# Gate products with the tokens as the stationary operand

## The chip, the core and the metric

The kernel runs on one core of one Trainium2 chip. The metric is the device time of one execution in microseconds. Five engines work side by side on a core, each through its own list of instructions in order: TensorE (PE, matrix products, with its weight loads shown apart as PEld), VectorE (DVE), ScalarE (ACT), GpSimd (POOL) and SyncE (SP, which issues DMAs). A matrix product holds one operand still in the array (the stationary one, which a weight load brings there) and streams the columns of the other through it. Before the change the median of three runs is 1689.38 us, from 1689.24 to 1691.82.

## The reference

Causal attention over 4 batches and 8 heads of 576 tokens, with a bias from cumulative sums; its output, 2304 tokens of 512 features, goes through a mixture of 8 experts whose weights per token come from gate logits that are balanced over rows and columns (Sinkhorn steps):

```
x = attn_out.transpose(0, 2, 1, 3).reshape(2304, 512)
logits = x @ w_gate                      # 512 x 8
P = exp(logits - logits.max())
repeat 8 times: P /= rows' sums; P /= columns' sums; P *= N / E
out = sum over e of P[:, e] * (relu(x @ w1[e]) @ w2[e])
```

## The kernel before

The program has two stages. In the attention stage, up to about 350 us, the 16 pairs of heads are worked off in 80 slots (a pair and a block of 128 query rows, the fifth of 64 rows for both heads). `st0` computes scores (tile `sc`, line 497), their row minimum on DVE (line 506) and the exponential on ACT (tile `T`, line 538); `st1` normalises `T` on ACT (line 560); `st2` transposes it on PE (tile `tr`, lines 569 and 579) and copies it out on DVE (lines 574 to 580); `st3` multiplies with v (tile `pv`, line 599). Line 615 on ACT writes its result as the high half of x (tile `xh`) and line 616 on DVE the low half. x is kept transposed, features on the partitions and tokens along the columns, and every value as a pair of a high and a low part.

Between the slots a queue (`Stream`, worked off by `fill`) puts in the first units of expert 0, for which x of a batch must be complete: products of line 148 and line 177, with results in two PSUM banks (tile `g`, taken by `bank`). Into this queue the gate is inserted, for two blocks of tokens per batch, eight blocks in all: six of 256 tokens and two of 384. Weights for the stream are loaded into `wraw` and split by line 110 on ACT (high part) and line 111 on POOL (low part).

The gate (`gate`, lines 620 to 633) has 16 columns in `wg`: the high and the low part of the 8 columns of w_gate. `gate` holds 16 columns of `wg` as the stationary operand and streams 256 or 384 tokens, 4 blocks of features by 2 parts of x, into a bank; ACT copies the 16 x 256 logits to `lt` (line 632). `gate_t` is queued two places later, transposes 16 x 128 pieces of `lt` on PE (line 641), and ACT copies the result to `lraw` (line 646), 128 tokens on the partitions. After the last block the Sinkhorn steps read `lraw` (line 795 on), beside the expert products of the second stage (lines 1024, 1145 and 1202), which take the rest of the time.

The order of the instructions on each engine is not the order of the code: a scheduler plans the whole program with its own estimate of what each instruction costs, and the stages' order on every engine comes out of that plan. The products of line 599 are the only ones with a raised priority.

Of the kernel before, what the change touches and what calls it, by code (L numbers as in the profile page):

```python
# [8 lines left out]
F32 = mybir.dt.float32  # L9
# [5 lines left out]
P = 128  # L15
# [8 lines left out]
KD = DM // P  # L24
# [21 lines left out]
def fused_kernel(ctx: ExitStack, tc: tile.TileContext, qT, kT, v, s, w_gate, wu, out):  # L46
    nc = tc.nc
# [8 lines left out]
    ident = const.tile([P, P], F32, name="ident")  # L56
    ones = const.tile([P, P], F32, name="ones")
    wg = const.tile([P, KD, 16], F32R, name="wg")
# [14 lines left out]
    def xgroup(b):  # L73
        if b not in xg:
            xg[b] = big.tile([P, 2, KD, GW], F32R, name="xh", tag="xh", bufs=2)
        return xg[b]

    def xcols(b, hl, k, n0, n):
        return xgroup(b)[:, hl, k, n0 - GB[b] : n0 - GB[b] + n]
# [57 lines left out]
    def bank():  # L137
        return cur["g"].tile([P, 512], F32, name=cur["gt"], tag=cur["gt"])
# [110 lines left out]
    stream = Stream()  # L249
# [71 lines left out]
    apool = actx.enter_context(tc.tile_pool(name="apool", bufs=1))  # L321
# [7 lines left out]
    def load_head(h):  # L329
        tag, bufs = ("raw", 4) if h else ("T", 7)  # L330
        for which, src in (("q", qT), ("k", kT)):
            r = (h - 2) % 5 - 2 if 2 <= h < 17 else -1
            if r < 0:
                raw = apool.tile([P, S], F32, name=f"raw{which}", tag=tag, bufs=bufs)
            else:
                if not rx:
                    rx.append(stage.tile([P, 6, S], F32, name="rx", tag="w7"))
                raw = rx[0][:, 2 * r + (which == "k")]
            eng = nc.scalar if h < 2 and which == "k" else nc.sync
            eng.dma_start(out=raw[:D], in_=src[h])  # L340
            heads_in[0] = eng.dma_start(out=raw[D:], in_=src[h])
            raws[h, which] = raw
# [139 lines left out]
    def load_v(g):  # L482
        b, hp = divmod(g, NPAIR)
        t = vtt[g % 2]
        src = v[b, :, hp * P : (hp + 1) * P]
        with tc.issue_after(heads_in[0].ins):
            nc.sync.dma_start(
                out=t[:, 0:4, :], in_=src[0:512].rearrange("(c p) d -> p c d", p=P)
            )
            nc.sync.dma_start(out=t[D:, 4, :], in_=src[512:576])  # L490
# [20 lines left out]
    def st0(t, j):  # L511

        g, i = t
        T = apool.tile([P, S], F32, name="T", tag="T", bufs=7)
        mn = apool.tile([P, 2], F32, name="mn", tag="mn", bufs=6)
        if j == 0:
            sums[t] = apool.tile([P, 2], F32, name="sm", tag="sm", bufs=4)
        if i < 4:
            n = (i + 1) * P
            sc = psa.tile([P, 512], F32, name="sc", tag="sc", bufs=3)  # L520
            scores(sc[:, :n], 2 * g + j, i, slice(0, n), True, True)
            m0 = 384 - i * P
            row_min(T[:, :n], sc[:, :n], mask[:, m0 : m0 + n], 3.0e38, mn[:, 1:2])
        else:
            n = S
            for pi in range(2):
                cols = slice(pi * 288, (pi + 1) * 288)
                sc = psa.tile([P, 512], F32, name="sc", tag="sc", bufs=3)
                for jj in range(2):
                    scores(sc[:, :288], 2 * g + jj, 4, cols, jj == 0, jj == 1)  # L530
                row_min(
                    T[:, cols],
                    sc[:, :288],
                    mask2 if pi else mask[:, :288],
                    mn[:, 0:1] if pi else 3.0e38,
                    mn[:, pi : pi + 1],
                )
        nc.scalar.activation(
            T[:, :n], T[:, :n], AF.Exp, bias=mn[:, 1:2], scale=-1.0,
            accum_out=sums[t][:, j : j + 1],  # L540
        )
        Ts[t, j] = T

    def heads(t):
        return range(2 if t[1] < 4 else 1)

    def st1(t):

        g, i = t
        sm = sums.pop(t)  # L550
        nh = len(heads(t))
        n = (i + 1) * P if i < 4 else S
        nc.scalar.activation(
            sm[:, :nh], sm[:, :nh], AF.Identity, bias=guard[:, 0:1], scale=1.0
        )
        rec = apool.tile([P, 2], F32, name="rec", tag="rec", bufs=2)
        nc.vector.reciprocal(out=rec[:, :nh], in_=sm[:, :nh])
        for j in heads(t):
            T = Ts[t, j][:, :n]
            nc.scalar.activation(T, T, AF.Copy, scale=rec[:, j : j + 1])  # L560
# [58 lines left out]

    def gate(b, n0, n):  # L620
        ps = bank()
        for k in range(KD):
            for x in range(2):
                nc.tensor.matmul(  # L624
                    ps[:16, :n],
                    lhsT=wg[:, k, :],
                    rhs=xcols(b, x, k, n0, n),
                    start=(k == 0 and x == 0),
                    stop=(k == KD - 1 and x == 1),
                )  # L630
        lt = apool.tile([16, 384], F32, name="lt", tag="lt", bufs=2)
        nc.scalar.copy(lt[:, :n], ps[:16, :n])
        lts[n0] = lt

    lts = {}

    def gate_t(n0, n):
        lt = lts.pop(n0)
        ps = bank()
        for c in range(n // P):  # L640
            nc.tensor.transpose(
                ps[:, c * 16 : (c + 1) * 16],
                lt[:, c * P : (c + 1) * P],
                ident[:16, :16],
            )
        nc.scalar.copy(
            lraw[:, n0 // P : (n0 + n) // P, :],
            ps[:, : n // P * 16].rearrange("p (c e) -> p c e", e=16),
        )
# [35 lines left out]
    def fill(ti):  # L685

        nxt = min([x for x in (23, 43, 63) if x > ti] + [NS + 3])
        budget[0] += len(stream.queue) / (2.0 * (nxt - ti))
        while budget[0] >= 0.5:
            stream.step()  # L690
            budget[0] -= 1.0
# [19 lines left out]
    for ti in range(NS + 3):  # L711
        if ti < NS:
            g, i = slots[ti]
            if i == 4 and g + 1 < NG:
                load_v(g + 1)
            for j in heads(slots[ti]):
                st0(slots[ti], j)
        if 1 <= ti <= NS:
            st1(slots[ti - 1])
        fill(ti)  # L720
        if 3 <= ti:
            pg, pi = slots[ti - 3]
            if pi == 1:
                st3(pg, (0, 1))
            elif pi == 4:
                st3(pg, (2, 3, 4))
        for j in range(2):
            if 2 <= ti < NS + 2 and j in heads(slots[ti - 2]):
                st2(slots[ti - 2], j)
            if j == 0:  # L730
                fill(ti)
        if ti < NS and i in (1, 3) and g + 1 < NG:
            h = 2 * (g + 1) + i // 2
            prep_head(h)
            ahead = {2: (4, 5), 3: (6,), 16: ()}.get(h, (h + (3 if h < 16 else 2),))
            for hh in ahead:
                if hh < B * H:
                    load_head(hh)
        gs = (ti - 7) // 5
        if ti >= 7 and slots[ti - 7][1] == 4 and gs >= NPAIR:  # L740
            spill(*divmod(gs, NPAIR))
        if ti in (24, 28, 32, 36):
            spill(0, (ti - 24) // 4)
        if ti == 6:
            gate_weights()
        if 4 <= ti < 18:
            u, r = divmod(ti - 4, 7)
            if r in (0, 3):
                with tc.issue_after(heads_in[0].ins):
                    w_load_early(u, (r // 3,))  # L750
            if r > 2:
                w_split_early(u, r - 3)
        prep(ti)
        if ti == 66:
            for i in range(2):
                nc.gpsimd.tensor_copy(
                    xgroup(3)[:, i, :, : EDGE[1] - EDGE[0]],
                    xgroup(2)[:, i, :, GB[3] - GB[2] : GB[3] - GB[2] + EDGE[1] - EDGE[0]],
                )

        for bb in range(B):
            if ti == (bb + 1) * 20 + 2:
                if bb < B - 1:
                    for k in range(4):
                        stream.add_visit(4 * bb + k, w_load_early, w_split_early)
                for x, (n0, n) in enumerate(EARLY[bb]):
                    stream.queue.insert(4 * x + 1, lambda b=bb, n0=n0, n=n: gate(b, n0, n))
                    stream.queue.insert(4 * x + 3, lambda n0=n0, n=n: gate_t(n0, n))
    for hp in range(NPAIR - 2, NPAIR):
        if 20 * (B - 1) + 5 * hp + 4 + 7 >= NS + 3:  # L770
            spill(B - 1, hp)
# [454 lines left out]
    k = 0  # L1226
# [161 lines left out]
```

## Time and profile before

| | |
|---|---|
| median of 3 runs | 1689.38 us |
| the profiled execution | 1689.67 us |
| its span, first to last instruction | 1687.9 us |
| PE busy | 1662.8 us (99%) |
| DVE, ACT, POOL busy | 1175.9, 833.9, 866.8 us |
| mean granted clock of PE | 0.992 of full speed |

Busy times come from records of single instructions. A product's record runs from its start to its modelled end, and the next one starts before that end, so how long a product holds PE is read from the distance between starts. The granted clock is the share of TensorE's full speed, 2.4 GHz, that was let through; it has two levels, 1.00 and 0.50. A row of the timeline gives the start, the time from the first start to the last end of a merged group, the engine, the line, the operation, what is written from what, the sizes, the count, and in brackets how long the engine sat idle before it and what ended that.

### The profile page before, as it was taken

The page shows a single profiled execution, that of the slowest core. Times are in us where ns is not written, and L with a number is a line of the kernel's source. Part 1 is how long each engine was busy: PE and PEld are TensorE (multiplying, and loading weights), DVE is VectorE, ACT ScalarE, POOL GpSimd, SP SyncE. Part 2 cuts the span into 40 slices and gives each one's busy share as a digit, 9 for nine tenths or more (in the row PEclk, how much of TensorE's full clock was granted, in tenths as well). Part 3 has the DMA queues.
Part 4 walks back from the last instruction along what each step waited for, and adds up shares of the span by engine and source line. Part 5 has one row for each costly group of instructions (what it writes and reads, how often), then busy time and mean ns, then how long its engine had stood idle before and what let it go on. Part 6 is the DMA issues. An engine that isn't in the chain of part 4 may idle for free.

```text
span 1687.9 us, 31232 instructions
## 1 busy us (share of the span) xinstructions
PE 1662.8 (99%) x11149; PEld 1568.2 (93%) x11149; DVE 1175.9 (70%) x2307; ACT 833.9 (49%) x1816; POOL 866.8 (51%) x797
## 2 busy tenths in 40 slices
PE   7899999999999999999999999999999999999998
PEld 6788898888899999999899999999999999999998
DVE  6677566665866766776457777777777778777666
ACT  5876766633544444444235444444445444444443
POOL 7658868432653554553314545554554555455543
PEclk8899999999999999999999999999999999999999
DMA  7677666283876866865966566666687666665652
GB/s 199 176 217 233 197 176 193 98 321 132 289 251 232 266 218 214 280 216 190 354 183 206 183 191 188 188 188 188 189 313 241 210 190 187 187 187 184 188 186 88
DMA packets 204699, 351.06 MB, mean 208 GB/s; under 512 B 21056, under 2 KB 102976, under 8 KB 204512
## 3 DMA queue, kind: packets, MB, share of 16 engines
q1 hardware_dynamic: 204064, 348.14, 64.5%
q8 instruction: 89, 1.46, 0.4%
q10 hardware_dynamic: 480, 0.92, 0.2%
q14 instruction: 66, 0.54, 0.1%
HBM read 248.89 MB, written 94.81 MB: 204 GB/s over the span
## 4 chain that ended last, share of the span: by engine, by line
PE 90%; DVE 4%; DMA 2%; ACT 1%; POOL 1%; issue 1%; SPq 1%; ACTq 0%; DVEq 0%; POOLq 0%
PE c L1024 34%; PE zz L1145 13%; PE zz L1202 13%; PE y L1202 10%; PE g L148 4%; PE g L177 4%; PE pv L599 3%; PE sc L497 3%; PE tr L569 2%; PE c L177 1%; PE c L148 1%; DVE s L999 1%; DMA wraw<-wu 1%; DVE h L252 1%; PE g L624 0%
## 5 line engine op out<-in xcount | busy, mean ns | idle before, releaser
L252 POOL TENSOR_TENSOR w2o<-r,w2o 128x512 fp32r<-128x512 f32 x189 | 272.4, 1462 | 282.0 <-ACT w2o L1182 273.4
L1202 PE MATMUL zz<-w2o,h 128*128 128x256 f32 x2016 | 272.8, 280 | 0.0
L1024 PE MATMUL c<-xS,w1o 128*128 128x384 f32 x1344 | 271.5, 336 | 1.0 <-ACT t L1039 0.6
L1202 PEld LDWEIGHTS zz<-w2o,h 128*128 128x128 f32 x2016 | 263.2, 188 | 0.2 <-POOL w2o L252 0.2
L1145 PE MATMUL zz<-w2p,h 128*128 128x512 f32 x1008 | 256.8, 391 | 0.4 <-ACT h L987 0.4
L988 DVE SCALAR_TENSOR_TENSOR h<-z,h 128x384 fp32r<-128x384 f32 x252 | 192.5, 769 | 66.0 <-ACT h L987 63.3
L987 ACT ACTIVATE h<-z 128x384 fp32r<-128x384 f32 x252 | 130.6, 525 | 205.3 <-DVE z L255 201.4
L1024 PEld LDWEIGHTS c<-xS,w1o 128*128 128x128 f32 x1344 | 227.3, 188 | 2.5 <-DVE z L255 1.2
L999 DVE SCALAR_TENSOR_TENSOR s<-z,s 128x384 f32<-128x384 f32 x224 | 180.4, 843 | 65.2 <-ACT s L1062 62.0
L252 POOL TENSOR_TENSOR h<-s,h 128x384 fp32r<-128x384 f32 x112 | 138.0, 1240 | 165.5 <-ACT h L995 164.8
L1145 PEld LDWEIGHTS zz<-w2p,h 128*128 128x128 f32 x1008 | 186.9, 188 | 29.5 <-ACT h L987 0.7
L1024 PE MATMUL c<-x,w1o 128*128 128x384 f32 x1008 | 202.9, 336 | 0.0
L1202 PE MATMUL y<-w2o,h 128*128 128x256 f32 x1512 | 201.7, 280 | 0.7 <-DVE a L1128 0.6
L1202 PEld LDWEIGHTS y<-w2o,h 128*128 128x128 f32 x1512 | 194.6, 188 | 1.5 <-DVE a L1128 1.0
L255 DVE TENSOR_TENSOR z<-c,t 128x384 f32<-128x384 f32 x252 | 136.7, 550 | 69.6 <-PE c L1024 65.5
L1024 PEld LDWEIGHTS c<-x,w1o 128*128 128x128 f32 x1008 | 170.5, 188 | 0.5
L1128 DVE SCALAR_TENSOR_TENSOR a<-zz,prob,a 128x256 f32<-128x256 f32 (+1 forms) x210 | 110.6, 530 | 67.1 <-PE zz L1202 52.4
L995 ACT CAST h<-s 128x384 fp32r<-128x384 f32 x224 | 110.9, 513 | 74.0 <-DVE s L999 69.0
L1024 PE MATMUL c<-xS,wp 128*128 128x384 f32 x672 | 134.5, 336 | 1.4 <-DVE z L255 1.4
L1182 ACT CAST w2o<-r 128x1024 fp32r<-128x1024 f32 x98 | 102.5, 1047 | 52.9 <-PE y L1202 39.5
L1024 PEld LDWEIGHTS c<-xS,wp 128*128 128x128 f32 x672 | 119.0, 188 | 9.6 <-DVE z L255 2.7
L252 POOL TENSOR_TENSOR wp<-s,wp 128x512 fp32r<-128x512 f32 x56 | 80.2, 1432 | 84.1 <-ACT wp L914 76.1
(149 smaller groups left out, 2727.5 us busy)
## 6 DMA issues: line engine op xcount, KB each, us to landing
w1o<-w1d SPq DMA_DIRECT2D x392, 256.0 KB
w1d<-wp SPq DMA_DIRECT2D x84, 512.0 KB
r<-wu SPq DMA_DIRECT2D x70, 512.0 KB
r<-w2d SPq DMA_DIRECT2D x56, 512.0 KB
sa<-wu SPq DMA_DIRECT2D x28, 512.0 KB
w2d<-sb SPq DMA_DIRECT2D x56, 256.0 KB
wraw<-wu SPq DMA_DIRECT2D x20, 512.0 KB
xS<-xd_S SPq DMA_DIRECT2D x12, 768.0 KB
```

The costliest lines, as they stand in the source:

```text
L148: nc.tensor.matmul(ps[:, :n], lhsT=w1[:, w, o : o + P], rhs=xcols(b, x, k, n0, n), start=(k == 0 and t == 0), stop=(k == KD - 1 and t == 2),)
L252: (eng or nc.gpsimd).tensor_tensor(out=out, in0=a, in1=b, op=ALU.subtract)
L255: (eng or nc.gpsimd).tensor_tensor(out=out, in0=a, in1=b, op=ALU.add)
L987: mark["a"] = nc.scalar.activation(t[:, 0], z, AF.Relu)
L988: mark["v"] = nc.vector.scalar_tensor_tensor(out=t[:, 1], in0=z, scalar=0.0, in1=t[:, 0].bitcast(F32), op0=ALU.max, op1=ALU.subtract,)
L995: nc.scalar.copy(t[:, 0], z)
L999: nc.vector.scalar_tensor_tensor(out=out, in0=z, scalar=0.0, in1=other, op0=ALU.max, op1=op)
L1024: mm = nc.tensor.matmul(ps, lhsT=w[:, wl, k], rhs=x[:, xl, k], start=(fresh and k == 0 and t == 0), stop=(k == 1 and t == 2), skip_group_c ...
L1128: nc.vector.scalar_tensor_tensor(out=a, in0=ps, scalar=prob[:, c, e : e + 1], in1=a, op0=ALU.mult, op1=ALU.add)
L1145: mm = nc.tensor.matmul(zb[ci], lhsT=h[:, a, ci * P : (ci + 1) * P], rhs=w[:, b_], start=(ui == 0 and f == 0 and t == 0), stop=(ui == UPE ...
L1182: nc.scalar.copy(w[:, :, 0], r)
L1202: nc.tensor.matmul(ps, lhsT=h[:, a, ci * P : (ci + 1) * P], rhs=w[:, ui, b_], start=(fresh and ui == 0 and t == 0), stop=(ui == UPE - 1 an ...
```

## The change

The operands of the gate's products change places: 128 tokens of x are the stationary operand, and the 16 columns of `wg` are streamed. The result has the tokens on the partitions already, so `lt`, its copy and the transposes go, and one copy per block brings the logits to `lraw`. In place of 8 products for a block there are 8 for each 128 tokens. The second entry in the queue goes too.

```diff
     def gate(b, n0, n):
         ps = bank()
-        for k in range(KD):
+        for c in range(n // P):
             for x in range(2):
-                nc.tensor.matmul(
-                    ps[:16, :n],
-                    lhsT=wg[:, k, :],
-                    rhs=xcols(b, x, k, n0, n),
-                    start=(k == 0 and x == 0),
-                    stop=(k == KD - 1 and x == 1),
-                )
-        lt = apool.tile([16, 384], F32, name="lt", tag="lt", bufs=2)
-        nc.scalar.copy(lt[:, :n], ps[:16, :n])
-        lts[n0] = lt
-
-    lts = {}
-
-    def gate_t(n0, n):
-        lt = lts.pop(n0)
-        ps = bank()
-        for c in range(n // P):
-            nc.tensor.transpose(
-                ps[:, c * 16 : (c + 1) * 16],
-                lt[:, c * P : (c + 1) * P],
-                ident[:16, :16],
-            )
+                for k in range(KD):
+                    nc.tensor.matmul(
+                        ps[:, c * 16 : (c + 1) * 16],
+                        lhsT=xcols(b, x, k, n0 + c * P, P),
+                        rhs=wg[:, k, :],
+                        start=(k == 0 and x == 0),
+                        stop=(k == KD - 1 and x == 1),
+                    )
         nc.scalar.copy(
             lraw[:, n0 // P : (n0 + n) // P, :],
             ps[:, : n // P * 16].rearrange("p (c e) -> p c e", e=16),
...
                 for x, (n0, n) in enumerate(EARLY[bb]):
                     stream.queue.insert(4 * x + 1, lambda b=bb, n0=n0, n=n: gate(b, n0, n))
-                    stream.queue.insert(4 * x + 3, lambda n0=n0, n=n: gate_t(n0, n))
```

The plan of the whole attention stage comes out differently from the first gate product on. Two places are shown. The first is ACT at the third pair of heads, about 58 to 64 us of the run before. `T_881` is the exponential of the pair's fifth block, `T_928` and `T_936` are the next pair's first; `w2_1006` is the weight part split from `wraw_923`, `xh_438` a piece of x. Before:

```order
L538 ACTIVATE T_963,sm_965<-T_963,mn_964 128x256
L553 ACTIVATE sm_930<-sm_930,guard_220 128x2
L615 CAST xh_438<-pv_902 128x256
L538 ACTIVATE T_971,sm_965<-T_971,mn_972 128x256
L110 CAST w2_1006<-wraw_923 128x512 x2
L538 ACTIVATE T_1009,sm_1011<-T_1009,mn_1010 128x384
L560 ACTIVATE T_881<-T_881,rec_944 128x576
L560 ACTIVATE T_928<-T_928,rec_979 128x128
L560 ACTIVATE T_936<-T_936,rec_979 128x128
```

And now, in the same place:

```order
L538 ACTIVATE T_963,sm_965<-T_963,mn_964 128x256
L553 ACTIVATE sm_930<-sm_930,guard_220 128x2
L538 ACTIVATE T_971,sm_965<-T_971,mn_972 128x256
L560 ACTIVATE T_881<-T_881,rec_944 128x576
L615 CAST xh_438<-pv_902 128x256
L110 CAST w2_1006<-wraw_923 128x512 x2
L560 ACTIVATE T_928<-T_928,rec_979 128x128
L560 ACTIVATE T_936<-T_936,rec_979 128x128
L553 ACTIVATE sm_965<-sm_965,guard_220 128x2
```

The normalising of `T_881` has moved ahead of the two weight casts and of the cast of `xh_438`. The second place is PE at the end of the attention stage, the last two blocks of the gate (256 and 384 tokens) with the expert products around them. Before:

```order
L148 MATMUL g<-xh,w_5164 128x256 x12
L624 MATMUL g<-xh,wg 16x256 x8
L641 MATMUL g<-ident,lt 128x16 x2
L624 MATMUL g<-xh,wg 16x384 x8
L641 MATMUL g<-ident,lt 128x16 x3
L177 MATMUL g<-w_5281,hh 128x512 x2
```

And now, where lines behind the gate have smaller numbers and its products are on line 625:

```order
L148 MATMUL g<-xh,w_5189 128x256 x12
L625 MATMUL g<-wg,xh 128x16 x40
L177 MATMUL g<-w_5306,hh 128x512 x2
L177 MATMUL g<-w_5306,hl 128x512
L177 MATMUL g<-w_5306,hh 128x512 x2
```

Sixteen and 24 products now stand in one row of 40, with nothing between. Behind them the order of PE, and from there on that of the other engines too, is the one of before to the end of the program. The row of 24 for the other block of 384 tokens stands alone in the middle of the attention stage.

## Rows read from the trace of the kernel before

**Rows 1.** The page's engines, and the granted clock in 40 slices, in tenths

```profile
PE 1662.8 (99%) x11149; PEld 1568.2 (93%) x11149; DVE 1175.9 (70%) x2307; ACT 833.9 (49%) x1816; POOL 866.8 (51%) x797
...
PEclk8899999999999999999999999999999999999999
```

**Rows 2.** Busy times of each engine by stretch, with count; granted clock, DMA

```profile
core 0: us, PE busy (x) PEld busy (x) DVE busy (x) ACT busy (x) POOL busy (x), PEclk, DMA share, GB/s
...
50.00:66.00 16.00, 11.62 (x93) 8.67 (x91) 9.99 (x38) 13.15 (x39) 12.20 (x13) 0.96 0.71 183
66.00:71.00 5.00, 5.00 (x52) 4.67 (x53) 1.44 (x8) 3.59 (x10) 0.00 (x0) 0.50 0.24 66
...
80.00:346.00 266.00, 265.90 (x2253) 237.23 (x2252) 173.96 (x542) 176.69 (x498) 174.09 (x241) 1.00 0.60 181
346.00:352.00 6.00, 4.99 (x33) 3.38 (x33) 1.05 (x4) 2.00 (x6) 0.00 (x0) 1.00 0.99 294
352.00:1687.00 1335.00, 1326.18 (x8403) 1273.04 (x8401) 949.07 (x1582) 599.15 (x1150) 635.17 (x477) 1.00 0.66 214
```

**Rows 3.** Tiles wg and lt: duration ns min/median/max, first and last start, forms

```profile
L624 PE MATMUL g<-xh,wg x64: 276/281/421, 51.8 to 349.5; 128*16 128x256 f32 x48, 128*16 128x384 f32 x16
...
L641 PEld LDWEIGHTS g<-ident,lt x18: 133/136/138, 83.7 to 350.5; 16*128 16x128 f32 x18
...
L632 ACT COPY lt<-g x8: 344/361/470, 81.6 to 349.9; 16x256 f32<-16x256 f32 x6, 16x384 f32<-16x384 f32 x2
```

**Rows 4.** Timeline of PE, 162 to 180 us: two gate blocks and what follows

```profile
164.67 1.11 PE L624 MATMUL g<-xh,wg 128*16 128x256 f32 x8
165.61 0.38 PE L569 MATMUL tr<-ident,T 128*128 128x128 f32 x2
...
171.63 1.65 PE L624 MATMUL g<-xh,wg 128*16 128x384 f32 x8
173.11 0.33 PE L497 MATMUL sc<-ka,qa 128*128 128x384 f32 x1
```

**Rows 5.** Timeline of PE, 346 to 351 us: the last two gate blocks

```profile
346.54 1.09 PE L624 MATMUL g<-xh,wg 128*16 128x256 f32 x8
348.08 0.29 PE L641 MATMUL g<-ident,lt 16*128 16x16 f32 x2 [0.45 <-ACT lt L632]
348.31 1.56 PE L624 MATMUL g<-xh,wg 128*16 128x384 f32 x8
350.43 0.35 PE L641 MATMUL g<-ident,lt 16*128 16x16 f32 x3 [0.56 <-ACT lt L632]
350.71 0.74 PE L177 MATMUL g<-w,hh 128*128 128x512 f32 x2
```

**Rows 6.** Timeline of the weight loads, at 263.6 and at 350.4 us

```profile
263.56 0.19 PEld L497 LDWEIGHTS sc<-ka,qa 128*128 128x128 f32 x1
263.67 0.19 PEld L497 LDWEIGHTS sc<-kb,qb 68*128 68x128 f32 x1
...
350.43 0.26 PEld L641 LDWEIGHTS g<-ident,lt 16*128 16x128 f32 x3 [0.97 <-ACT lt L632]
```

**Rows 7.** Timeline of ACT, 61 to 74 us, where it idles or catches up

```profile
61.54 1.14 ACT L110 CAST w<-wraw 128x512 fp32r<-128x512 f32 x2 [1.21 <-DMA wraw<-wu]
...
63.19 1.34 ACT L560 ACTIVATE T<-T,rec 128x576 f32<-128x576 f32 x3
...
70.28 0.37 ACT L615 CAST xh<-pv 128x256 fp32r<-128x256 f32 x1 [1.26 <-PE pv L599]
...
73.13 0.21 ACT L615 CAST xh<-pv 128x64 fp32r<-128x64 f32 x1 [2.28 <-DVE xh L616]
```

**Rows 8.** Timeline of PE: a wait, and line 599 at two clocks

```profile
64.00 0.66 PE L569 MATMUL tr<-ident,T 128*128 128x128 f32 x4 [1.59 <-ACT T L560]
...
67.04 3.20 PE L599 MATMUL pv<-at,vt 128*64 128x128 f32 x28
...
81.17 1.70 PE L599 MATMUL pv<-at,vt 128*64 128x128 f32 x28
```

## The prediction

> **What bounds the kernel now.** I read the page's list of engines first, and its slices of the clock. TensorE (PE) is busy 99% of the span and no other engine comes near [rows 1]. A share over the whole span hides the stages, so next I took the busy times by stretch [rows 2]. From 80 to 346 us, the second half of the attention, PE is busy 265.90 of 266 us; ACT is busy 176.69 of the same 266. From 352 us on, the expert products, PE is busy 1326 of 1335 us. The 16 us from 50 to 66 are different: PE is busy 11.6 of them, ACT 13.2. And from 66 to 71 us PE is busy all the time, but at a granted clock of 0.50, the lower of its two levels, 1.2 GHz; the slices show the same dent. So two questions decide. How much PE time do the gate products need after 80 us, where each microsecond is one of the total? And what becomes of the stretch from 50 to 80 us, where PE waits for ACT and then runs slowly?
>
> **What is removed.** The gate has 64 products, 48 with 256 streamed columns and 16 with 384, 18 transposes and 8 copies on ACT [rows 3]. A duration in that list is a latency and not the time that PE is held, so I take distances between starts. Eight products of 256 columns last from 164.67 to 165.61, where the next instruction starts: 0.94 us, 118 ns each. Eight of 384 last from 171.63 to 173.11, 1.48 us [rows 4]. Six blocks of the first kind and two of the second make 6 x 0.94 + 2 x 1.48 = 8.6 us. The transposes of a block hold PE 0.23 us (348.08 to 348.31) or 0.28 us (350.43 to 350.71) [rows 5]: 6 x 0.23 + 2 x 0.28 = 1.9 us. In the last two blocks nothing stands between the products and their transposes, and PE waits for ACT's copy: 348.08 - 346.54 - 0.94 = 0.60 us and 350.43 - 348.31 - 1.48 = 0.64 us [rows 5]. Together 8.6 + 1.9 + 1.2 = 11.7 us of PE time. The eight ACT copies, 8 x 0.361 = 2.9 us, I count at nothing: after 80 us ACT has 89 idle microseconds under PE [rows 2].
>
> **What is added.** There are 18 groups of 128 tokens with 8 products each, 144 products. Each streams 16 columns, but first loads 128 columns of x as its stationary operand. The columns streamed fall from 48 x 256 + 16 x 384 = 18432 to 2304, so what counts is how densely loads can follow one another. Before has no such product in this number format. The nearest row is two loads of 128 x 128 in the score products, where the streams between are short: they start at 263.56 and 263.67, 0.11 us apart [rows 6]. Lower bound: the gate's transposes also load 128 columns and stream 16; three of their loads are done in 0.26 us, where one takes 0.136, which leaves (0.26 - 0.136) / 2 = 0.062 us from one to the next [rows 3, 6]. Upper bound: a load that overlaps nothing takes its whole recorded 0.19 us [rows 6]. So 144 products cost 8.9 to 27.4 us, and I take 0.11, the same kind of load: 15.8 us. Against the 11.7 removed PE does 4.1 us more (2.8 less to 15.7 more at the bounds). The tail itself hardly changes: the last 40 products need 40 x 0.11 = 4.4 us, where products, waits and transposes took 346.54 to 350.71, 4.17 us [rows 5]. The logits go to the Sinkhorn steps at the same place, behind one copy as before. From there on the order of all engines is the old one, so the 1335 us that follow should only shift.
>
> The Trainium skill ("TensorE: Matmul & The Clock Gate", Back-to-back issue gap) lists products of 1 to 64 columns at about 60 cycles, some 25 ns. By that figure alone 144 products would be an estimated 3.6 us, and the change would save 8 us. The trace speaks against using it here: loads stand 0.11 us apart [rows 6], and here each product has a load of its own. No run before shows a product of 16 columns that needs no load, so the figure itself stays untested.
>
> **What is moved.** The order is planned for the whole program, so other gate costs reshuffle all engines from 52 us to the end of the attention. The place that matters is ACT near 60 us. There, in before, a pair of weight casts (line 110) waits 1.21 us for its DMA until 61.54, and the normalising copies of line 560, T_881 first, stand behind it and start at 63.19 [rows 7]. PE's next transposes need T_881 and wait 1.59 us, to 64.00 [rows 8]. Then the granted clock falls: the 28 products of line 599 that start at 67.04 take 3.20 us, where 28 at the full clock take 1.70 [rows 8]. ACT in turn idles 1.26 us for these products and 2.28 us behind them [rows 7]. Now T_881 is normalised ahead of the casts, and PE has its transposes earlier. What is late next? The cast of xh now stands behind T_881's copy, and the gate's product on PE waits for it; T_881 is one of three copies that took 1.34 us [rows 7], so that is about 0.6 us, and the casts still wait for the DMA until 61.54. Some waiting on PE is thus left, and the clock may fall here all the same. But ACT, which sets the pace of this stretch, would find the products of line 599 done when it comes to them. The two idle times of ACT, 1.26 + 2.28 = 3.5 us, are what can be won. Bounds: 0, if the idle time only moves, and 3.5 plus PE's wait, 5.1 us. I take 3.3, near the two rows of ACT, because behind the casts ACT has a queue of ready work.
>
> **The sum.** 4.1 more on PE, 3.3 won ahead of it: +0.8 us. The profiled execution took 1689.67 us, its span of 1687.9 and 1.8 around it, and stands 0.3 above the median of 1689.38. 1689.67 + 0.8 = 1690.5 us. 0.2%, 3.4 us, is about what a measurement of this kernel can tell from no change, so this is "the same".
>
> **Rivals.**
> First, slower: the clock falls behind the new gate blocks. The last block is 40 products in a row, 4.4 us in which PE loads almost all the time and streams 640 columns; another has 24. In before the clock stayed at 1.00 from 346 to 352, with 0.6 us waits in it [rows 2, 5], but there 8 x 256 + 8 x 384 = 5120 columns were streamed in the place of these 640, so this speaks for neither side. What speaks for it: before 66 us, with PE partly idle, the clock did fall. Whether loading alone keeps it up no row of before tells. The price by the row: 5 us at 0.50 [rows 2] lose 2.5 us. Two such stretches, behind the 40 and behind the 24, cost 5 us: 1690.5 + 5 = 1695.5. It decides as soon as one stretch of 5 us or more is at 0.50 beyond the one that before has.
>
> Second, slower by little: nothing is won at 60 us, since another wait on ACT or DMA takes the place of the old one. Then 1689.67 + 4.1 = 1693.8. For it: all orders there are new, and ACT waits for DMAs that do not come sooner. Against it: 3.5 us of ACT's idle time hang on slow PE work that is now free earlier.
>
> Third, faster: loads follow at the spacing of the gate's transposes or closer. At 0.062 us, 8.9 for all, PE does 2.8 us less than before, and with the 3.3 won the time is 1689.67 - 6.1 = 1683.6. Against it: the load of 128 x 128 in this format is recorded at 0.19 us, that of the transposes at 0.136 [rows 3, 6]. The page's 25 ns go the same way and have no chance beside this one.
>
> **How the numbers follow.** My forecast 0.54, the falling clock 0.30, nothing won 0.10, cheap loads 0.06. Slower by over 0.2%: 0.27 of the second (a single stretch would leave it the same), 0.05 of the third (its 1693.8 is near the border of 1692.8), none of the first: 0.32. Faster: 0.06 and 0.02 of mine, 0.08. The same: 0.60. The forecast's own range is 1688.7 to 1692.8, with 5.1 won at the one end and 1 at the other. For 8 times in 10 I go to 1687 below, as the cheap loads have little weight, and to 1696 above, which takes in the falling clock at its price.
>
> **What would show it.** On PE, eight gate products in a row should take about 0.88 us and the 40 at the end 4.4; if they take 0.5 or 1.5, the sum of loads is wrong. ACT's idle time between 62 and 75 us should be near nothing, and the products of line 599 there come some 3 us earlier. The granted clock after 80 us should be 1.00 throughout; any stretch at 0.50 behind a gate block is the first rival. From the last gate block on PE to the end of the span the distance should be what it was, 1687.9 - 350.71 = 1337.2 us. If that distance changes by over 1 us, the claim that the rest only shifts is wrong.

## The result and the profile after

The changed kernel takes 1698.88 us in the median of 6 runs (1697.14 to 1702.93), the kernel before 1689.52 us beside it (1687.97 to 1691.82). The ratio is 1.0056, with a 95% interval from 1.0045 to 1.0067: slower by 9.4 us, where "the same", 1690.5, was forecast. It lies above the predicted range, 1687 to 1696. The profiled execution took 1699.04 us, its span is 1697.2, 9.3 longer than that of before.

The page's engines and clock of the changed kernel, beside [rows 1]:

```profile
PE 1673.1 (99%) x11211; PEld 1581.9 (93%) x11211; DVE 1180.1 (70%) x2307; ACT 832.8 (49%) x1808; POOL 866.4 (51%) x797
...
PEclk7999999989999999999999999999999999999999
```

The share of PE is still 99%, but the clock's ninth slice, 339 to 382 us, has a dent that before did not have. Busy times by stretch of the changed kernel, columns as in [rows 2], with the stretches cut where the granted clock changes:

```profile
50.00:66.00 16.00, 14.50 (x152) 12.45 (x150) 11.85 (x45) 14.34 (x43) 12.81 (x14) 0.89 0.78 198
55.60:58.90 3.30, 3.30 (x18) 2.86 (x18) 2.86 (x13) 3.27 (x12) 3.14 (x4) 0.50 0.90 218
66.00:71.00 5.00, 4.15 (x41) 3.53 (x37) 4.04 (x18) 4.73 (x14) 3.92 (x6) 1.00 0.71 200
...
171.00:174.00 3.00, 3.00 (x32) 2.83 (x28) 1.27 (x7) 2.52 (x9) 2.92 (x4) 1.00 0.82 242
175.10:178.40 3.30, 3.30 (x13) 2.91 (x12) 1.78 (x5) 0.06 (x1) 3.30 (x8) 0.50 0.80 242
178.50:349.00 170.50, 170.50 (x1414) 153.44 (x1413) 107.56 (x323) 106.25 (x291) 105.78 (x152) 1.00 0.52 156
349.00:352.50 3.50, 2.44 (x23) 2.35 (x21) 1.26 (x3) 1.48 (x4) 0.80 (x1) 1.00 0.97 317
352.60:362.70 10.10, 9.01 (x33) 8.24 (x34) 5.16 (x9) 2.28 (x6) 6.68 (x6) 0.50 1.02 415
362.80:1697.00 1334.20, 1325.61 (x8399) 1272.59 (x8397) 942.93 (x1575) 596.43 (x1144) 627.38 (x471) 1.00 0.65 212
```

The stretch from 66 to 71 us, at 0.50 before, now runs at 1.00; in its place the clock is at 0.50 from 55.6 to 58.9, so for about 3.4 us where it was 6.8 (64.9 to 71.7). Behind 80 us two stretches are new at 0.50: 175.1 to 178.4, right behind the row of 24 gate products, with PE busy all the time; and 352.6 to 362.7, around the last gate block. Where they begin and end is seen on PE's timeline of the changed kernel, which answers [rows 4, 5, 8]:

```profile
65.13 1.70 PE L599 MATMUL pv<-at,vt 128*64 128x128 f32 x28
...
78.69 1.70 PE L599 MATMUL pv<-at,vt 128*64 128x128 f32 x28
...
171.31 2.83 PE L625 MATMUL g<-wg,xh 128*128 128x16 f32 x24
173.99 0.44 PE L569 MATMUL tr<-ident,T 128*128 128x128 f32 x2
...
349.59 1.85 PE L625 MATMUL g<-wg,xh 128*128 128x16 f32 x16
353.69 5.29 PE L625 MATMUL g<-wg,xh 128*128 128x16 f32 x24 [2.25 <-DVE hl L159]
358.83 1.20 PE L177 MATMUL g<-w,hh 128*128 128x512 f32 x2
```

The 28 products of line 599 that took 3.20 us at 67.04 [rows 8] take 1.70 at 65.13; one pair of heads later the lead is 81.17 - 78.69 = 2.48 us. The 24 gate products take 173.99 - 171.31 = 2.68 us, 0.112 each. But the 40 at the end are no single row. After 16 of them PE stands still 2.25 us for `hl` on DVE, and the other 24 take 358.83 - 353.69 = 5.14 us, 0.214 each, at the lower clock.

Why PE waits for `hl` stands on ACT and DVE. ACT of the changed kernel (the first two rows answer [rows 7]):

```profile
60.53 0.76 ACT L560 ACTIVATE T<-T,rec 128x576 f32<-128x576 f32 x1
...
62.13 1.14 ACT L110 CAST w<-wraw 128x512 fp32r<-128x512 f32 x2 [0.58 <-DMA wraw<-wu]
...
351.00 0.62 ACT L899 CAST wp<-sa 128x512 fp32r<-128x512 f32 x1 [3.80 <-DMA sa<-wu]
351.53 0.38 ACT L158 ACTIVATE hh<-g 128x256 fp32r<-128x256 f32 x1
```

DVE of the changed kernel:

```profile
351.20 0.69 DVE L252 TENSOR_TENSOR s<-sa 128x512 f32<-128x512 f32 x1 [2.15 <-DMA sa<-wu]
351.98 1.32 DVE L252 TENSOR_TENSOR s<-s,sa 128x256 f32<-128x256 f32 x1
353.22 0.41 DVE L159 SCALAR_TENSOR_TENSOR hl<-g,hh 128x256 fp32r<-128x256 f32 x1
```

And ACT and DVE of the kernel before at the same place:

```profile
346.74 0.38 ACT L158 ACTIVATE hh<-g 128x256 fp32r<-128x256 f32 x1 [2.57 <-PE g L148]
...
351.60 0.62 ACT L914 CAST wp<-sa 128x512 fp32r<-128x512 f32 x1 [0.58 <-DMA sa<-wu]
...
347.15 0.43 DVE L159 SCALAR_TENSOR_TENSOR hl<-g,hh 128x256 fp32r<-128x256 f32 x1 [1.15 <-ACT hh L158]
```

Before, `hh` is made as soon as its products are done, and the first weight cast of the second stage (`wp` from `sa`) comes 4.9 us later. In the new plan this cast and two subtractions of line 252 stand ahead of the last `hh` and `hl`. Casts and subtractions wait for a DMA that lands at 351.0 us (351.6 in the kernel before). So ACT idles 3.80 us, and `hh`, whose products are done when the gate's start at 349.59, begins at 351.53; `hl` follows behind the subtractions and is done at 353.63. The second gate block takes the PSUM bank (tile `g`) that this `hl` reads, and starts at 353.69.

**The balance.** Last products of line 599 of the attention: 341.36 us before, 344.40 after, +3.04. That is 104 gate products and what they replace, +3.9; 3.4 us at half the clock behind the 24, +1.7; and so, by the difference, -2.56 from the stretch before 80 us, which the 2.48 above agrees with. End of the attention, up to the first product of line 177 behind the gate: 358.83 - 349.59 = 9.24 us where 4.17 stood [rows 5], +5.07. Of these 9.24, 4.4 are 40 x 0.11, 2.25 the standstill, 2.5 the half clock. Behind it the half clock lasts to 362.78, and the distance to the end is 1697.2 - 358.83 = 1338.4 in the place of 1337.2, +1.2. In sum 3.04 + 5.07 + 1.2 = 9.3.

### The profile page after: what moved, and what is told of

Its sections match the earlier page's. It is cut to its first block, busy times and chain, and to the rows that moved or that the text cites. A ratio compares the mean times of both kernels' runs of the same rounds, so it can differ in the third digit from the quotient of the medians.

```text
span 1697.2 us, 31351 instructions
## 1 busy us (share of the span) xinstructions
PE 1673.1 (99%) x11211; PEld 1581.9 (93%) x11211; DVE 1180.1 (70%) x2307; ACT 832.8 (49%) x1808; POOL 866.4 (51%) x797
## 4 chain that ended last, share of the span: by engine, by line
PE 91%; DVE 4%; DMA 1%; SPq 1%; issue 1%; POOL 1%; ACT 1%; DVEq 0%; ACTq 0%; POOLq 0%
PE c L1009 34%; PE zz L1130 13%; PE zz L1187 13%; PE y L1187 10%; PE g L177 4%; PE g L148 4%; PE sc L497 3%; PE pv L599 3%; PE tr L569 2%; PE c L148 2%; PE c L177 2%; DVE s L984 1%; PE g L625 1%; DMA wraw<-wu 1%; DVE h L252 1%
```

## The experiments

The ratios are to the kernel before, whose medians beside the runs were 1688.3 to 1689.6 us. Single executions of one kernel differ by up to 7.5 us, so the times are compared by their intervals, and of a profile only stretches with stretches. A profile is one execution, and where the clock falls in it is read from that one alone.

**One part of the change at a time.** The new gate for batches 0 to 2 alone (`gate_o` is the old one):

```diff
-    stream.queue.insert(4 * x + 1, lambda b=bb, n0=n0, n=n: gate(b, n0, n))
-    stream.queue.insert(4 * x + 3, lambda n0=n0, n=n: gate_t(n0, n))
+    if bb < B - 1:
+        stream.queue.insert(4 * x + 1, lambda b=bb, n0=n0, n=n: gate(b, n0, n))
+    else:
+        stream.queue.insert(4 * x + 1, lambda b=bb, n0=n0, n=n: gate_o(b, n0, n))
+        stream.queue.insert(4 * x + 3, lambda n0=n0, n=n: gate_t(n0, n))
```

> The change for the first three batches alone; the last two gate blocks keep the old products, copy and transposes. The plan up to there is the one of the changed kernel, the tail's that of the kernel before. Theory A (the loss is 3.9 us more PE time against 2.5 won near 65 us, a fall of the clock behind the 24 products, 1.7, and a tail that costs 5 to 7 us): the tail's part goes, about 3.0 us over the kernel before, 1692.5; one stretch of 3.4 us at 0.50 near 175 us stays, none behind 340. Rival B (the clock falls in the tail because PE stands still there for 2.25 us, not because few columns are streamed, and the fall at 175 is an accident): the same time, but no stretch at 0.50 behind 80 us need appear.

1692.99 us, ratio 1.0022 [1.0012, 1.0033]. The clock falls at 173.7 us for 3.4 us and not again. And for the last batch alone (`if bb == B - 1`):

> The change for the last batch alone: the last 40 products in the new form, the six blocks before in the old one. Plan up to the tail as before, the tail as in the changed kernel, with ACT's and DVE's preparation of weights, which waits for a DMA, ahead of the last hh and hl. A and B alike: PE stands still for about 2 us between the 16 and the 24 products, and the clock falls to 0.50 there; 5 to 7 us over the kernel before, 1694.5 to 1696.5. If the tail's loss came from the different plan ahead of it, this would be within 2 us of before.

1695.10 us, 1.0033 [1.0018, 1.0049]. PE of this kernel:

```profile
344.88 1.85 PE L656 MATMUL g<-wg,xh 128*128 128x16 f32 x16
348.90 5.29 PE L656 MATMUL g<-wg,xh 128*128 128x16 f32 x24 [2.17 <-DVE hl L159]
```

So 3.4 and 5.5 us, 8.9 together, which agrees with the 9.4 within their intervals: the larger part is in the last batch, and it needs nothing of the change in the others.

**The order at the end.** The changed kernel, with the casts of the second stage held behind the last copy to `lraw` on ACT, and the first subtractions behind the last `hl` on DVE:

```diff
-        nc.scalar.copy(hi, src)
+        with tc.issue_after(held_a.ins):      # the last copy to lraw
+            nc.scalar.copy(hi, src)
...
-            sub(
+            with tc.issue_after(held_v.ins):  # the last hl
+              sub(
```

> The changed kernel with one edit: ACT's first weight casts of the next stage stand behind the last copy of the logits, and DVE's first subtraction behind the last hl, so that nothing of the tail's gate waits for a DMA. PE's order stays that of the changed kernel, 40 products in a row. Theory A (few streamed columns let the clock fall): no standstill in the 40, but the clock falls to 0.50 behind or within them all the same, and some 2 to 3 us of the 9.4 come back: 1696 to 1697. Rival B (the standstill lets it fall): clock 1.00 in the tail, the 40 products take 4.4 us, 6 to 7 us come back: 1692.5.

1694.13 us, 1.0030 [1.0018, 1.0042]. PE, and busy times around it:

```profile
350.27 4.53 PE L626 MATMUL g<-wg,xh 128*128 128x16 f32 x40
```

```profile
350.00:355.60 5.60, 5.60 (x48) 5.47 (x47) 2.46 (x6) 1.33 (x5) 0.00 (x0) 1.00 0.99 352
355.70:359.00 3.30, 3.30 (x9) 2.39 (x8) 1.52 (x3) 1.72 (x4) 3.30 (x4) 0.50 1.00 418
```

The 40 are one row of 4.4 us, 0.110 each, and the time comes down by 4.75 us. The order on ACT and DVE is thus worth half the loss. A shorter fall, 3.4 us, remains behind the 40, as behind the 24. The time lies between what the two theories expected, since both have a part.

**More columns.** The changed kernel, with `wg` widened to 128 columns by copies (the first 16 are used), so that each product streams 128 in the place of 16:

```diff
-                        ps[:, c * 16 : (c + 1) * 16],
+                        ps[:, c * P : (c + 1) * P],
```

> The changed kernel with 128 streamed columns for each gate product in the place of 16 (the 16 repeated eight times, the copy takes the first 16): the same 144 loads, eight times the columns. The plan ahead of the tail hardly differs; in the tail hh stands ahead of the weight casts, as in the kernel before. Loads set the pace, so a product should still take 0.11 us. Theory A: the clock stays at 1.00 from 80 us to the end and the time is before + 3.9 - 2.5, about 1691. Rival B: no standstill in the tail, so no fall there, but the fall behind the 24 products near 175 us stays: 1692.6. If 128 columns cost more than the load (0.2 us each), 1703.

1691.29 us, 1.0012 [1.0003, 1.0022]. PE:

```profile
349.63 4.58 PE L625 MATMUL g<-wg,xh 128*128 128x128 f32 x40
```

Eight times the columns, the same 0.110 us for each product (354.05 - 349.63 = 4.42 for 40), and no stretch at 0.50 from 62 us to the end. It is 7.6 us faster than the changed kernel. But its plan puts `hh` ahead of the cast again, so it takes away the standstill too, and does not tell the two apart.

**The standstill by itself.** The wide kernel, with the last `hl` computed ten times:

```diff
+            for _ in range(10 if (b, u, n0, f) == (2, 3, 1408, 1) else 1):
                 nc.vector.scalar_tensor_tensor(
```

> 128 columns streamed by each gate product, and the last low part of h computed ten times on DVE, so that PE stands still about 2 us between its 16 and its 24 last gate products, as it does in the changed kernel. Theory A (few streamed columns let the clock fall, the standstill alone does not): no stretch at 0.50 after 80 us, time of the kernel with 128 columns plus 3 to 4 us, 1694 to 1695. Rival B (the standstill drops the clock whatever streams): a stretch of 3 to 10 us at 0.50 from 352 us on, 1696 to 1699.

1693.45 us, 1.0029 [1.0018, 1.0040], no fall. But the plan gave the second gate block the other bank, and PE stood still only 0.28 and 0.29 us. This tells nothing of a standstill of 2 us, so it was made again, with the other bank also late:

```diff
+        for _ in range(20 if b == B - 1 and n == 256 else 1):
             nc.scalar.copy(
                 lraw[:, n0 // P : (n0 + n) // P, :],
```

> 128 columns streamed by each gate product. In the last batch the first block's copy to lraw is made 20 times on ACT and the last low part of h ten times on DVE, so that both PSUM banks come free late and PE stands still 2 to 3.5 us between its 16 and its 24 products, as long as in the changed kernel or longer. Theory A (what PE does ahead of the standstill decides: few streamed columns let the clock fall, wide ones do not): no stretch at 0.50 from 340 us on, the time of the kernel with 128 columns plus the standstill, 1693.5 to 1695.5. Rival B (the standstill itself drops the clock): a stretch at 0.50 of 3 to 10 us behind it, 1695.5 to 1700.

1698.75 us, 1.0056 [1.0042, 1.0070]. PE, and busy times:

```profile
348.14 1.90 PE L626 MATMUL g<-wg,xh 128*128 128x128 f32 x16
353.36 5.38 PE L626 MATMUL g<-wg,xh 128*128 128x128 f32 x24 [3.32 <-DVE hl L159]
```

```profile
352.60:362.60 10.00, 9.24 (x34) 8.37 (x35) 3.03 (x7) 3.19 (x13) 3.03 (x3) 0.50 0.32 123
```

This is the picture of the changed kernel, with 128 columns. My theory that the few columns alone make the clock fall is wrong for the end of the attention: a standstill of 3.32 us, behind products of 128 columns, is followed by the same 10.2 us at 0.50.

**Shorter rows.** The changed kernel, with one queue entry for each 128 tokens, so that the 24 become three rows of 8 with other work between:

```diff
-    stream.queue.insert(4 * x + 1, lambda b=bb, n0=n0, n=n: gate(b, n0, n))
+    for c in range(n // P - 1, -1, -1):
+        stream.queue.insert(4 * x + 1 + 2 * c,
+            lambda b=bb, n0=n0, c=c: gate(b, n0 + c * P, P))
```

> The changed kernel with one queue entry for each 128 tokens: the 24 gate products near 171 us are then three runs of 8 with other products between; at the end the 40 stand together or nearly so. Theory A (only a long run of few-column products lets the clock fall): no stretch at 0.50 near 175 us, 1.7 us less than the changed kernel, about 1697; the fall at the end remains. Rival B (the fall at 175 comes from another cause of that place, such as the order of the other engines): it stays at 3.4 us, time about 1698.9.

1697.77 us, 1.0057 [1.0044, 1.0070]. No stretch at 0.50 between 60 and 351 us, as expected; the time is not told from that of the changed kernel. At the end five blocks share two banks, PE waits 3.2 us for two copies to `lraw` (2.0 and 1.2), and the clock falls for 10.2 us.

**Other banks.** The changed kernel, with the gate's results in the banks of the transposes:

```diff
-        ps = bank()
+        ps = psa.tile([P, 512], F32, name="tr", tag="tr", bufs=2)
```

> The changed kernel, its 16 columns and its order on ACT and DVE at the end kept, but the gate's results go to the two banks of the transposes (tile tr), not to the two of the stream (tile g). Theory (PE stands still since the second gate block needs the bank that the last low part of h still reads): the wait of 2.25 us between the 16 and the 24 products goes, one of the same length may come back at the product of line 177 that reads this low part; a fall of the clock behind the 40 stays. 1694 to 1697. Rival (PE waits for something else of that place, such as the copy on ACT): the wait stays in the gate products, 1698.9.

1695.64 us, 1.0048 [1.0033, 1.0064]. PE:

```profile
349.01 2.86 PE L625 MATMUL tr<-wg,xh 128*128 128x16 f32 x25
...
354.32 0.39 PE L177 MATMUL g<-w,hl 128*128 128x512 f32 x1
356.97 0.27 PE L788 MATMUL y<-ident,mx 128*1 128x128 f32 x1 [2.26 <-DVE mx L785]
358.17 4.42 PE L148 MATMUL c<-xh,w 128*128 128x256 f32 x19 [0.93 <-DVE acc L188]
```

The wait is gone from the gate, so it was the bank. But it comes back where PE needs the first reduction of the Sinkhorn steps, as long as it was: its input, the last copy to `lraw`, stands behind casts on ACT, at 354.75, and behind it DVE takes 1.13 us for line 780 and puts 0.6 us of line 188 ahead of the reduction, at 356.63. From 357.4 the clock is at 0.50 for 6.8 us. Here neither the 24 products in the middle nor these 25 were followed by a fall, which left the part of the columns open.

**Long rows.** So the 24 near 171 us were made four times over, 96 in a row, of which the last pass counts, in the changed kernel and in the wide one:

```diff
+        for _ in range(4 if n == 384 and b < B - 1 else 1):
             for c in range(n // P):
```

> The changed kernel, with the 24 gate products near 171 us made four times over (96 in a row, the last pass being the one that counts), 16 columns streamed by each. Theory A (a row of few-column products lets the clock fall, and where a row of 24 does not, it was too short for the place where it lies): the clock falls to 0.50 inside the row or right behind it, for 6.8 us or more in all; the 96 take 13 to 20 us in the place of 96 x 0.11 = 10.6. Rival C (the falls after 171 us come from something else of that place): the row takes 10.6 us, and a fall behind it is 3.4 us or none. The end as in the changed kernel in either case.

> The same 96 products in a row, each with 128 columns streamed. Theory A: the row takes 96 x 0.111 = 10.7 us at a clock of 1.00, and there is no fall behind it. Rival C (the number of columns does not matter): the same clock as in the kernel with 16 columns, 13 to 20 us for the row or a fall behind it. Against the kernel with 128 columns and no repeats: 72 x 0.111 = 8.0 us more, about 1699.

1712.72 us (1.0147 [1.0118, 1.0177]) and 1699.32 (1.0064 [1.0041, 1.0087]). Busy times with 16 columns:

```profile
172.00:177.30 5.30, 5.30 (x52) 5.23 (x48) 1.12 (x6) 2.36 (x9) 5.16 (x9) 1.00 0.80 226
177.40:190.90 13.50, 13.50 (x59) 12.89 (x59) 0.56 (x1) 0.20 (x1) 10.99 (x24) 0.50 0.57 177
```

With 128 columns, the same stretches:

```profile
172.00:177.30 5.30, 5.30 (x51) 5.30 (x49) 0.74 (x4) 1.98 (x8) 5.16 (x10) 1.00 0.84 241
177.40:190.90 13.50, 13.50 (x102) 12.95 (x102) 5.28 (x15) 4.39 (x14) 8.80 (x18) 1.00 0.57 181
```

PE is busy to 100% in both, loads weights to 95% and more in both, and nothing stands still. With 16 columns the clock is at 0.50 for 13.7 us, and the row takes 187.93 - 172.15 = 15.78 us; with 128 it stays at 1.00, 182.54 - 171.79 = 10.75 us. Between these two kernels the columns decide, as theory A said.

**The gain before 80 us, without the change.** The kernel before, with two of ACT's weight casts held behind the normalising of `T_881` (the lines that hold them):

```diff
+                    def hi(dst, src):
+                        with tc.issue_after(normed[2, 4].ins):
+                            return nc.scalar.copy(dst, src)
```

> The kernel before, gate untouched; only the two weight casts of ACT near 60 us are held behind the normalising of T_881. Theory (the early gain of the changed kernel comes from this order alone, not from the gate): the products of line 599 at 67 us start 1.4 us earlier and run at the full clock, the last such products of the attention start 2 to 2.5 us earlier, at 338.9 to 339.4 us, and the time falls to about 1687.2. Rival (the gain comes with the gate's own removal from PE and ACT): no change, 1689.6.

1690.11 us, 1.0007 [0.9998, 1.0016]: nothing won. The profiled execution took 1692.79 us, the longest of its 11. DVE and PE of it:

```profile
69.00 2.36 DVE L422 CAST ka<-rx 128x576 fp32r<-128x576 f32 x2
```

```profile
66.42 1.70 PE L599 MATMUL pv<-at,vt 128*64 128x128 f32 x28
...
71.85 0.38 PE L497 MATMUL sc<-ka,qa 128*128 128x256 f32 x1 [2.12 <-DVE mn L506]
```

The 28 products run at the full clock, 0.6 us earlier than in [rows 8]. Then PE waits 2.12 us for a row minimum that stands on DVE behind two casts of `ka`; these take 2.36 us here, 0.98 in the kernel before. Why they are slow is not shown; POOL works on line 428 beside the first of them (68.94 to 70.21), in the kernel before only from 72.53 on. In this kernel, too, `T_881` is normalised only at 62.65 us, in the changed one at 60.53. But this execution came late to the place: at 54.97 PE waits 1.58 us for a DMA (`qb`), 0.8 in the kernel before and 0.4 in the changed one. So the time says that the held casts win nothing; what the place of `T_881` is worth, this profile cannot say. The rival's time came true, its reason is not shown.

Two kernels were to beat the one before. Both put the old gate products of the last two blocks one behind the other, and chunks of line 177 ahead of their transposes, whose results go to the banks of tile `tr` (the last argument, 1):

```diff
+    stream.queue[at:at] = [lambda: gate(B - 1, a0, an), lambda: gate(B - 1, b0, bn)]
+    stream.queue[at + 4 : at + 4] = [lambda: gate_t(a0, an, 1), lambda: gate_t(b0, bn, 1)]
```

One of them has the held casts besides, the other the new gate in batch 0 alone.

> The kernel before with the early order of ACT and, for the last batch, the two blocks of gate products one behind the other with two chunks of line 177 between them and their transposes. Theory: the early 2 to 2.5 us and the two waits of 0.60 and 0.64 us on PE go, 1686.0 to 1686.8. Rival (the plan of the tail shifts a new wait in, as in the changed kernel): the tail gives nothing or loses, 1687.5 to 1691.

> The kernel before with the new form in the first batch alone (two blocks of 256, 32 products), the old form in the other three, and in the last batch the two old blocks one behind the other with chunks of line 177 ahead of their transposes. Theory (the early gain hangs on the whole new order near 60 us and stays where PE's cost does not): 32 x 0.11 against 2 x 1.17 on PE, 1.2 more; 2.5 won near 60 us; about 1.1 won at the end: 2.4 below the kernel before, about 1687.2. No stretch at 0.50 after 80 us. Rival (what is won near 60 us is given back before 120 us, as in the kernel with the held casts): 1689 to 1690.

1690.42 us, 1.0008 [0.9999, 1.0016], and 1689.05 us, 1.0001 [0.9992, 1.0009]. The two waits of 0.6 us at the end do go, and a new one of 0.5 us on DVE's `m` comes behind them in both. Neither beats the kernel before; both times are those of the rivals.

## Why the prediction was wrong

**The removed work, 11.7 us, and the price of a product, 0.11.** Right. The new products stand 0.107 to 0.112 us apart on the mean (80.52 to 81.52 for 9, 85.72 to 87.43 for 16), and 128 columns cost no more than 16. PE's 4.1 us more are there. That the load sets the pace is seen at the head of a row, where the product ahead holds the first one up and the load of the second catches up. In the changed kernel the first starts at 349.59; the second, and in the kernel with 128 columns the second behind 349.63:

```profile
349.62 0.37 PE L625 MATMUL g<-wg,xh 128*128 128x16 f32 x2
...
349.70 0.39 PE L625 MATMUL g<-wg,xh 128*128 128x128 f32 x2
```

So the second follows after 0.03 us with 16 columns and 0.06 with 128, and those behind it after 0.11 with either. The Trainium skill's 25 ns for a product of few columns ("TensorE: Matmul & The Clock Gate", Back-to-back issue gap), which that section gives for a product taken by itself, is near the 0.03 us of that second product and near no other distance in the row.

**The stretch before 80 us.** 3.3 was taken, 2.5 came in the profile. What was forecast is there: `T_881` at 60.53, the products of line 599 at the full clock (1.9 us earlier, not some 3), 0.58 us of waiting for the DMA in the place of 1.21. But that the new order wins the 2.5 is not shown. In the kernel with the last batch alone, PE, ACT and DVE have the order of the kernel before up to 346 us, and yet its profile shows:

```profile
60.90 1.14 ACT L110 CAST w<-wraw 128x512 fp32r<-128x512 f32 x2 [0.52 <-DMA wraw<-wu]
...
79.51 1.70 PE L599 MATMUL pv<-at,vt 128*64 128x128 f32 x28
```

The wait for the DMA is 0.52 us here too, the clock is at 0.50 for 3.4 us in the place of 6.8, and the lead at the second pair of heads is 81.17 - 79.51 = 1.66 us, two thirds of the 2.48, with the old order. The kernel with 128 columns does take only 1.65 us more than the one before, with 4.1 us more on PE; from this one may estimate 2.4 us won, 0.4 to 3.6 by its interval. With the casts held, nothing is won. So there may be a gain, and its cause is open.

**"The tail itself hardly changes."** This is the step that failed. The sum of products was right, 40 x 0.11 = 4.4 us. But it stood on the claim that "from there on the order of all engines is the old one". That was looked at behind the gate on PE; ACT and DVE had a new order just ahead of it, a cast and two subtractions that wait for a DMA in front of `hh` and `hl`, and keep another order than before up to about 400 us; PE stood still 2.25 us for `hl`, and the clock fell. The sign given for it, the distance from the last gate block to the end, changed by 1.2 us, just over the 1 us named; most of the loss lies ahead of it, inside the block, where 9.24 us stand in the place of 4.17. The run with the old order on ACT and DVE gives 4.75 us back, the one with other banks 3.24.

**The clock.** The forecast gave a fall behind the 40 and the 24 a chance of 0.30 and a price of 5 us. It came at both places. Behind the 24 it costs 1.7, in the place of 2.5. At the end it is another event: without the standstill (the kernel with the old order) 10.2 us at 0.50 become 3.4, and with a standstill of 3.32 us 128 columns do not prevent them. It costs 2.5 inside the gate and, it seems, the 1.2 behind it, beside the 2.25 of standing still. That the clock fell "with PE partly idle" before 66 us was the row that bore on it, and it was used only for loads.

**What stays open.** Rows of 24 or 25 products with 16 columns were followed by a fall in three profiles (the changed kernel, the one with batches 0 to 2, the one with the old order) and not in two places of the kernel with other banks; what decides there no run tells. How much of the 10.2 us in the changed kernel comes from its columns, beside the standstill, is not separated either. A fall may also come in one execution of a kernel and not in another: of the five of the kernel with other banks, the mean granted clock goes from 0.994 (1695.30 us) down to 0.988 (1701.08). And the 2.5 us of early gain are read from single profiles: with the new gate in batch 0 alone, the times show none.

## What to carry to other kernels

Making a stationary operand of the long side turns few loads into many: count the loads, and look at what they stream, since a long row of loads with few columns behind each can lose the clock while PE looks fully busy. When a plan is made anew, read the order of every engine that feeds the place, ahead of it as well as behind: a cast and two subtractions that wait for a DMA in front of ready instructions cost about as much here (4.75 us) as all the added work of PE (4.1). Price a wait on PE with the slow stretch that can follow it, which here cost more than the wait. And before a gain is read from one profile, look at a second execution of the same order: here it showed two thirds of the gain without the change.

## What the hardware showed that was not expected

A row of 96 products of 16 columns, each with its own load of 128 columns, ran at 0.50 from its 5.2nd microsecond on, with PE busy 13.50 of 13.50 us; the same row with 128 columns stayed at 1.00. Several standstills of PE were followed by 0.50 whatever had streamed: 2.12 us (3.4 us at 0.50), 2.25 (10.2), 2.26 and 0.93 (6.8), 3.32 (10.2); the two waits of 0.6 us in the kernel before were not [rows 5]. Nor was one of 2.05 us in the kernel with the new gate in batches 0 to 2, where the clock stays at 1.00 up to 173.7 us, so a standstill of 2 us does not always bring the lower clock:

```profile
55.70 0.30 PE L497 MATMUL sc<-kb,qb 68*128 68x128 f32 x1 [2.05 <-DMA qb<-qa]
...
55.70:62.00 6.30, 4.72 (x37) 3.61 (x37) 3.63 (x16) 6.27 (x22) 6.07 (x5) 1.00 0.86 235
```

At 0.50 a product with 16 columns takes 0.214 us, twice the 0.107 to 0.112, so the load, too, runs at the granted clock.
